# A table of steps for a four-segment attention and feed-forward kernel, with new first statistics, a new last inverse and a new last projection

## The chip, the core and the metric

The kernel runs on one core of a Trainium2 chip. Such a core has five engines with queues of their own that work in order and wait for each other through semaphores: TensorE (PE in the profile, with PEld for its weight loads), VectorE (DVE), ScalarE (ACT), GpSimd (POOL) and SyncE (SP, which here only issues DMAs). Operands lie in SBUF, 128 partitions wide. Products of TensorE go to PSUM, whose tiles VectorE and ScalarE read. The metric is the device time of one execution in microseconds (us).

## The reference

One sequence of 2048 rows and 448 columns is normalised row by row, and two branches read the result: an attention with a memory (16 heads of 28 columns, four segments of 512 rows), and a gated feed-forward layer with 1792 hidden columns. Inside a segment the attention is causal. The memory `M, z` is the sum over the segments before.

```
xn = layernorm(x)
for s in range(4):                          # per head, q, k, v = xn @ wq, wk, wv
    p = softmax(q_s k_s^T * scale + mask);  a_dot = p @ v_s
    a_mem = (phi(q_s) @ M) / (phi(q_s) @ z + 1e-6)      # phi(t) = t + 1 if t > 0 else exp(t)
    o_s = g * a_mem + (1 - g) * a_dot                   # g = sigmoid(beta), per head
    M += phi(k_s)^T v_s;  z += sum(phi(k_s))
s = concat(o_s) @ wo
out = x + s * silu((gelu(xn @ w_gate) * (xn @ w_up)) @ w_down)
```

## The kernel before

Everything is written out in one order by hand (a manual schedule), so the order in the code is each engine's order. A segment has four blocks of 128 rows (`b`), and its 16 heads are four groups (`g`) of four heads, each head padded from 28 to 32 partitions.

**Gate phases.** `gate_up(s)` runs over 14 chunks of 128 hidden columns. Each chunk is eight products into one of the two `ps_s` tiles, then a GELU on ScalarE (L511) and a product on VectorE (L512) that frees the tile. After each chunk the steps stand that a dictionary `table` gives for its number: statistics (`stats`, L241), scaling and transposing of the next segment, reading the memory (`memory_read`, L441), inverses of denominators (`invert`), and `scale_memory` and `combine`, which use them.

**Attention stages.** `attention(s, fill, at, lead)` takes a group in three steps (`BANKS`): key block 0 (512 query columns), key blocks 1 and 3 together (384 + 128 columns), and key block 2 alone (256 columns). A step is score products (L397), two exponentials on ScalarE (L403), masks of the diagonals on GpSimd (L407), and, two steps later, the products with the values (L418). Between steps a list `fill` of other TensorE work is dealt out by planned costs: projections of the next segment (L314, L352), the down projection (L523), and the products with `wo` (`finish_units`, L552). `at` gives steps to run at fixed half steps. `later(n, fn)` puts VectorE's half of a piece n ticks back.

**Inverses.** A group's accumulator is copied to SBUF (`evac`, L431). A DMA (L435) gathers the denominators of all groups into a small tile `dc`. `invert` computes the reciprocals there, splits each into three bf16 terms (L449 to L456), and three DMAs (L457) write these to `rows`. A product with a constant matrix `spread` (L465) then repeats every inverse over its head's partitions, and VectorE multiplies (L470, L481). In the last segment, groups 0 to 2 are inverted together, and group 3 afterwards, by the same way.

**The end.** After segment 3's attention the rest of its down projection runs, then the `wo` products of groups 0 to 2 for all four row blocks into two double tiles (L728), group 3's inverse and combination, its `wo` products, and per block a product (L738), an addition (L740) and a DMA out. In segments 0 to 2 GpSimd adds `x` and issues the output's DMA (L559, L560).

**The start.** 78 products of zeros (L93) run before the first data is there. VectorE takes the statistics of segment 0 (L241), GpSimd the power -1/2 (L247), VectorE scales, TensorE transposes (L265), ScalarE copies, and the value projection (L352) and then the key and query projections (L314) follow. `guard` squares the weights and sums the columns' squares by eight products (L218); a flag from this chooses the general path, which does not run here.

## Time and profile before

| what | value |
|---|---|
| median of 3 runs | 273.7 us (271.87 to 273.88) |
| the profiled execution's own time | 273.37 us |
| span in its trace, first to last instruction | 271.6 us |
| busy share of the span: PE, DVE, ACT, POOL | 92%, 70%, 57%, 37% |
| mean granted TensorE clock | 0.981 |

The span leaves 1.8 us of the execution's own time outside. The stages follow each other in the span: the start to 10.2 us, projections of segment 0 to 20.4, gate phase 0 to 45.0, attention 0 to 76.4, gate phase 1 to 103.5, attention 1 to 137.0, gate phases 2 and 3 to 187.0, attention 2 to 220.0, attention 3 to 245.6, and the end. The borders are read by eye from the chain of work, so a stage's edge can hold some of the next stage's instructions. Records of matmuls overlap, so a busy share of PE near one can still hold short waits.

### The profile page before, as it was taken

Reading aid. Unit: us, or ns where it says so; the run is one execution under the profiler, and the core shown is the slowest. Engines: PE = TensorE matmul, PEld = TensorE weight load, DVE = VectorE, ACT = ScalarE, POOL = GpSimd, SP = SyncE. Lnnn points to the kernel's source line nnn. Section 1 sums busy time; section 2 is a strip of 40 time slices with the busy share of each in tenths; the row PEclk is TensorE's granted clock in tenths of the full one; section 3 lists DMA queues with packets and bytes.
Section 4 is the critical chain, followed back from the end, with each engine's and each line's share of the span. In section 5 each row is a group of like instructions: output and inputs, shape, how many; then the busy total and the mean of one; then the engine's idle time right before and its main releaser. Section 6 shows DMA issues by size and latency. Waiting matters only on the chain.

```text
span 271.6 us, 4546 instructions
## 1 busy us (share of the span) xinstructions
PE 249.3 (92%) x1630; PEld 104.5 (38%) x1630; DVE 190.0 (70%) x371; ACT 155.5 (57%) x226; POOL 100.2 (37%) x203
## 2 busy tenths in 40 slices
PE   7899999999999999999999999999899998995940
PEld 7543334433333335444434333344333333332410
DVE  5876977667686878577778646355878756876862
ACT  2546735788985335688963332625887687871100
POOL 2100410455521400966622205121776563658011
PEclk9999999999999999999999999999999999999795
DMA  7999026020110143101110310002000010001002
GB/s 221 393 277 213 0 41 154 12 23 19 23 22 6 34 85 113 22 18 39 40 37 0 63 24 0 4 6 72 18 21 21 5 29 8 4 1 57 19 7 75
DMA packets 26358, 15.11 MB, mean 56 GB/s; under 512 B 17880, under 2 KB 25048, under 8 KB 26328
## 3 DMA queue, kind: packets, MB, share of 16 engines
q1 hardware_dynamic: 23032, 9.96, 16.7%
q10 hardware_dynamic: 2720, 3.40, 3.9%
q0 software_dynamic: 576, 1.38, 1.5%
q8 instruction: 15, 0.25, 0.4%
q14 instruction: 15, 0.12, 0.2%
HBM read 9.18 MB, written 1.84 MB: 41 GB/s over the span
## 4 chain that ended last, share of the span: by engine, by line
PE 66%; DVE 16%; ACT 6%; DMA 5%; issue 3%; POOL 1%; SPq 1%; DVEq 0%; ACTq 0%
PE s L496 22%; PE m L523 11%; PE m L314 9%; PE s L503 5%; PE s L397 5%; PE m L352 4%; PE pv L418 3%; ACT pt L403 3%; PE m L465 2%; DMA x_sb<-in_A_x_dram 2%; PE m L552 2%; DVE hT L512 2%; DMA rows<-terms 2%; PE m L441 1%; DMA dc<-oU 1%
## 5 line engine op out<-in xcount | busy, mean ns | idle before, releaser
L403 ACT ACTIVATE pt<-s 128x1024 bf16<-128x1024 f32 (+1 forms) x96 | 79.2, 885 | 16.8 <-PE s L397 16.3
L407 POOL TENSOR_SCALAR_AFFINE_SELECT pt<-pt 128x256 bf16<-128x256 bf16 x128 | 54.6, 449 | 71.5 <-ACT pt L403 70.0
L511 ACT ACTIVATE gl<-s 128x512 bf16<-128x512 f32 x56 | 33.4, 597 | 55.5 <-PE s L496 28.7
L512 DVE TENSOR_TENSOR hT<-gl,s 128x512 bf16<-128x512 bf16 x56 | 38.4, 685 | 31.4 <-ACT gl L511 31.3
L523 PE MATMUL m<-wd_sb,hT 128*128 128x448 bf16 x224 | 52.3, 361 | 0.9 <-DVE wu_sb L470 0.9
L496 PE MATMUL s<-xnT,wg_sb 128*128 128x512 bf16 x168 | 45.7, 381 | 1.2 <-DVE hT L512 1.2
L496 PE MATMUL s<-xnT,wu_sb 128*128 128x512 bf16 x168 | 45.4, 379 | 0.0
L523 PEld LDWEIGHTS <-hT 128*128 128x128 bf16 x224 | 20.7, 99 | 23.6 <-issue 6.8
L496 PEld LDWEIGHTS <-wu_sb 128*128 128x128 bf16 x168 | 16.4, 98 | 19.8
L397 PE MATMUL s<-qT,kT 32*128 32x512 bf16 (+3 forms) x256 | 20.9, 301 | 2.6 <-ACT pt L403 2.3
L496 PEld LDWEIGHTS <-wg_sb 128*128 128x128 bf16 x168 | 14.1, 97 | 22.2 <-issue 9.7
L247 POOL TENSOR_TENSOR rstd<-rstd,nhalf 128x2 f32<-128x2 f32 x8 | 5.7, 712 | 45.7 <-DVE rstd L245 45.7
L503 PE MATMUL s<-xnT,wg_sb 64*128 64x512 bf16 x112 | 19.4, 384 | 0.4 <-DVE hT L512 0.4
L318 DVE CAST kT<-m 128x512 bf16<-128x512 f32 x16 | 11.0, 688 | 11.2 <-PE m L314 11.0
L418 PE MATMUL pv<-pt,vaug 128*32 128x512 bf16 (+3 forms) x256 | 17.3, 307 | 0.0
L314 PE MATMUL m<-xnT,wk_pad 128*128 128x512 bf16 x64 | 17.1, 380 | 0.0
L314 PE MATMUL m<-xnT,wq_pad 128*128 128x512 bf16 x64 | 16.8, 380 | 0.2 <-DVE vaug L354 0.2
L397 PEld LDWEIGHTS <-kT 32*128 32x128 bf16 x256 | 6.5, 91 | 23.4 <-issue 23.1
L526 ACT ACTIVATE th<-m 128x448 f32<-128x448 f32 x16 | 8.8, 548 | 11.3 <-PE m L523 11.1
L352 PE MATMUL m<-wv_sb,xnT 128*128 128x448 bf16 x64 | 14.1, 352 | 0.6 <-DVE wu_sb L431 0.3
L465 PE MATMUL m<-rows,spread 128*128 128x512 bf16 x28 | 11.0, 391 | 3.1 <-DMA rows<-terms 2.6
L431 DVE COPY oU<-pv 128x512 f32<-128x512 f32 x13 | 8.9, 688 | 4.8 <-PE pv L418 4.8
(102 smaller groups left out, 305.7 us busy)
## 6 DMA issues: line engine op xcount, KB each, us to landing
x_sb<-in_A_x_dram SPq DMA_DIRECT2D x7, 224.0 KB
wd_sb<-in_B_w_down_dram SPq DMA_DIRECT2D x1, 1568.0 KB
wg_sb<-in_B_w_gate_dram SPq DMA_DIRECT2D x1, 1344.0 KB
wu_sb<-in_B_w_up_dram ACTq DMA_DIRECT2D x1, 1344.0 KB
out_dram<-o_out POOLq DMA_DIRECT2D x12, 112.0 KB, 2.1
xr<-in_A_x_dram ACTq DMA_DIRECT2D x2, 448.0 KB
wo_sb<-in_A_wo_dram SPq DMA_DIRECT2D x4, 98.0 KB
dc<-oU SPq DMA_DIRECT2D x24, 8.0 KB
```

Source lines behind the costliest of these rows:

```text
L314: nc.tensor.matmul(out=pr[:], lhsT=wpad[nm][:, c, g * HG:(g + 1) * HG, :].rearrange("p h d -> p (h d)"), rhs=xnT[s][:, c, :], start=(c == ...
L352: nc.tensor.matmul(out=vp[:, 0:D], lhsT=xnT[s][:, c, b * P:(b + 1) * P], rhs=wv_sb[:, c, :], start=(c == 0), stop=(c == NDC - 1))
L397: nc.tensor.matmul(out=sp[i // 2][:, i % 2, c0:c0 + n], lhsT=kT[s][r, g, kb * P:(kb + 1) * P], rhs=qT[s][r, g, kb * P:L], start=True, stop ...
L403: nc.scalar.activation(out=pt[:, :, 0:w], in_=sp[pr][:, :, 0:w], func=ACT.Exp, scale=scale)
L407: nc.gpsimd.affine_select(out=v, in_=v, pattern=[[0, 2], [1, P]], compare_op=ALU.is_ge, fill=0.0, base=0, channel_multiplier=-1)
L418: nc.tensor.matmul(out=acc[i * HP:(i + 1) * HP, kb * P:L], lhsT=va[:, kb, g * HG + i, :], rhs=pts[i // 2][:, i % 2, c0:c0 + n], start=(kb ...
L465: nc.tensor.matmul(out=r[:], lhsT=spread[:, g, :], rhs=rows[side][:], start=True, stop=True)
L496: nc.tensor.matmul(out=gu[:, i, :], lhsT=w_sb[:, c, cols], rhs=xnT[s][:, c, :], start=start and c == 0, stop=stop and c == NDC - 2)
L503: nc.tensor.matmul(out=gu[:, i, :], lhsT=wg_sb[rs, NDC - 1, cols], rhs=xnT[s][rs, NDC - 1, :], start=start, stop=stop)
L511: nc.scalar.activation(out=gl[:], in_=gu[:, 0, :], func=ACT.Gelu_apprx_tanh)
L512: nc.vector.tensor_tensor(out=hT[s][:, fc, :], in0=gl[:], in1=gu[:, 1, :], op=ALU.mult)
L523: nc.tensor.matmul(out=d_ps[:, 0:D], lhsT=hT[s][:, fc, b * P:(b + 1) * P], rhs=wd_sb[:, fc, :], start=(fc == 0), stop=(fc == NFC - 1))
```

## The change

One dictionary `PLAN` now says at which slot each named step runs. A slot is a gate chunk, a half step of an attention, or a unit of the last down projection; slots 0 to 13 are gate phase 0, 14 to 33 attention 0, 34 to 47 gate phase 1, 48 to 67 attention 1, 68 to 95 gate phases 2 and 3, 96 to 115 attention 2, 116 to 135 attention 3, and 136 onwards the end. Pairs such as `"v2": (0.031, 1.05)` say over which part of an attention a list of fill is spread, and other entries set delays and leads.

Beside the table:

- Two groups of heads share five attention steps instead of taking three each: the 256-column blocks of both go into one step. An attention has 10 steps, all 1024 columns wide for the exponentials.
- At the start ScalarE takes the statistics of blocks 2 and 3, GpSimd their power; 44 zero products instead of 78; `wv` is loaded before `wq`; memsets of `vaug` go to GpSimd; the value projection stands between the transposes.
- `guard` adds the squares on GpSimd, so that two products remain of eight; they stand in attention 0.
- Additions of `x` and output DMAs of segments 0 to 2 go from GpSimd to VectorE and SyncE. Three of the four `wo` units of segment 2 stand after attention 3.
- The last group's inverse: four f32 products with `pick` bring the denominators to the rows' partitions, VectorE inverts and spreads them, and four f32 products with `unit` turn them back. Its memory part is no longer added in `combine` but enters `wo` as a fifth source `om`.
- The last `wo` products run block by block, and GpSimd adds three of the four blocks.

```diff
+PLAN = {
...
+    "end30": 137, "end31": 137, "inv3": 138, "inv3l": 139, "cmb00": 42, "cmb10": 78, "cmb20": 126,
...
-        for i in range(78):
+        for i in range(44):
...
-                for c in range(NDC):
-                    nc.tensor.matmul(out=np_[0:1, 0:D], lhsT=ones[:], rhs=sqs[nm][:, c, :],
-                                     start=(c == 0), stop=(c == NDC - 1))
+                nc.tensor.matmul(out=np_[0:1, 0:D], lhsT=ones[:], rhs=sqs[nm][:, 0, :],
+                                 start=True, stop=True)
...
+            def stats_scalar(b):
+                junk = work.tile([P, D], BF16, name="ph_e")
+                nc.scalar.activation(out=junk[:], in_=xs[:, b, :], func=ACT.Copy, accum_out=mv[:, b, 0:1])
+                nc.scalar.activation(out=mv[:, b, 0:1], in_=mv[:, b, 0:1], func=ACT.Copy, scale=-1.0 / D)
+                nc.scalar.activation(out=junk[:], in_=xs[:, b, :], func=ACT.Square, bias=mv[:, b, 0:1],
+                                     accum_out=mv[:, b, 1:2])
...
-        BANKS = (((0, 0),), ((1, 0), (3, 384)), ((2, 0),))
+        STEPS = []
+        for a in range(0, G, 2):
+            b = a + 1
+            STEPS += [[(a, 0, 0)], [(a, 1, 0), (a, 3, 384)], [(a, 2, 0), (b, 2, 256)],
+                      [(b, 0, 0)], [(b, 1, 0), (b, 3, 384)]]
...
+        def invert_last():
+            o_a, d = oU[NSEG - 1, G - 1, 0], ps_m.tile([P, NB, HG], F32, name="m")
+            for b in range(NB):
+                nc.tensor.matmul(out=d[:, b, :], lhsT=o_a[:, b * P:(b + 1) * P], rhs=pick[:],
+                                 start=True, stop=True)
+            nc.vector.reciprocal(out=lden[:], in_=d[:])
...
+        def combine_last():
+            o_a, r = oU.pop((NSEG - 1, G - 1, 0)), ps_m.tile([P, L], F32, name="m")
+            for b in range(NB):
+                nc.tensor.matmul(out=r[:, b * P:(b + 1) * P],
+                                 lhsT=linv[:, b, :], rhs=unit[:], start=True, stop=True)
+            for h in range(2):
+                c = slice(h * L // 2, (h + 1) * L // 2)
+                nc.vector.tensor_tensor(out=oT[NSEG - 1][:, G - 1, c], in0=o_a[:, c], in1=r[:, c],
+                                        op=ALU.mult)
...
-                    nc.gpsimd.tensor_tensor(out=o_out[:], in0=t, in1=xr[s][:, b, :], op=ALU.add)
-                    nc.gpsimd.dma_start(out=o_v[s][:, b, :], in_=o_out[:])
+                    nc.vector.tensor_tensor(out=o_out, in0=t, in1=xr[s][:, b, :], op=ALU.add)
+                    nc.sync.dma_start(out=o_v[s][:, b, :], in_=o_out)
...
+        rest = d3[x:]
+        n = plan["fin_at"]
+        rest[n:n] = fin[w:]
...
-        for g in range(G - 1):
-            wo_part(g)
-        combine(3, G - 1, 1)
-        wo_part(G - 1)
+        combine_last()
+        srcs = [(om[0], G - 1)] + [(oT[3][:, g, :], g) for g in range(G)]
+        for b, a, z in ((0, 0, G), (1, 0, G), (0, G, G + 1), (1, G, G + 1), (2, 0, G + 1), (3, 0, G + 1)):
+            for n in range(a, z):
+                src, g = srcs[n]
+                nc.tensor.matmul(out=acc[b // 2][:, b % 2, 0:D], lhsT=src[:, b * P:(b + 1) * P],
+                                 rhs=wo_sb[:, g, :], start=(n == 0), stop=(n == G))
...
-            add = nc.vector if b % 2 else nc.gpsimd
+            add = nc.gpsimd if b < 3 else nc.vector
```

How the instructions stand now, at three places. A row is line, operation, output, inputs and shape; numbers behind a name tell buffers apart.

ScalarE at the start, after its table load, before (`oT` holds the raw `wk` here, `wu_sb` is the up weight, `m` a PSUM tile):

```order
L68 DMA oT<-in_A_wk_dram 128x3x448
L69 DMA oT<-in_A_wk_dram 64x448
L138 DMA wu_sb<-in_B_w_up_dram 128x3x1792
L139 DMA wg_sb<-in_B_w_up_dram 64x1792
L120 COPY wq_pad<-oT 128x64x28
L266 COPY xnT<-m 128x4x128 x4
```

ScalarE at the same place, in the changed kernel (`mv` holds mean and variance):

```order
L91 DMA oT_169<-in_A_wk_dram 128x3x448
L92 DMA oT_169<-in_A_wk_dram 64x448
L321 ACTIVATE ph_e_211,mv_204<-x_sb_105 128x448
L322 ACTIVATE mv_204<-mv_204 128x1
L323 ACTIVATE ph_e_211,mv_204<-x_sb_105,mv_204 128x448
L321 ACTIVATE ph_e_215,mv_204<-x_sb_105 128x448
```

The up weight's DMAs left this queue for SyncE's, the statistics of block 2 and then 3 came in, and the padding of `wq` went behind the copies of the transposes.

ScalarE in attention 2, four steps in the middle, before (`pt` are the exponentials, `s` the scores):

```order
L403 ACTIVATE pt_2570<-s_2564 128x1024
L403 ACTIVATE pt_2573<-s_2565 128x1024
L403 ACTIVATE pt_2615<-s_2605 128x1024
L403 ACTIVATE pt_2619<-s_2606 128x1024
L403 ACTIVATE pt_2650<-s_2644 128x2x256
L403 ACTIVATE pt_2653<-s_2645 128x2x256
L403 ACTIVATE pt_2674<-s_2668 128x1024
L403 ACTIVATE pt_2677<-s_2669 128x1024
```

ScalarE in attention 2 of the changed kernel, steps in the middle:

```order
L489 ACTIVATE pt_2536<-s_2530 128x1024
L489 ACTIVATE pt_2539<-s_2531 128x1024
L489 ACTIVATE pt_2577<-s_2567 128x1024
L489 ACTIVATE pt_2581<-s_2568 128x1024
L489 ACTIVATE pt_2620<-s_2610 128x1024
L489 ACTIVATE pt_2624<-s_2611 128x1024
```

The narrow pair is gone: two of them, from two groups, make one pair of full width.

VectorE's last rows before (`oU0_3198` is group 3's accumulator, `wg_sb` the feed-forward factor of segment 3, `s` the sums of `wo` products, `wv_sb` the output):

```order
L530 SCALAR_TENSOR_TENSOR wg_sb_2333<-th_3266,m_3250 128x448
L481 TENSOR_TENSOR oU0_3198<-oU0_3198,m_3283 128x512
L482 TENSOR_TENSOR oT_3208<-oU0_3198,wu_sb_2334 128x512
L738 TENSOR_TENSOR wg_sb_2333<-wg_sb_2333,s_3269 128x448 x2
L740 TENSOR_TENSOR wv_sb_3291<-wg_sb_2333,x_sb_1369 128x448
L738 TENSOR_TENSOR wg_sb_2333<-wg_sb_2333,s_3270 128x448 x2
```

VectorE's last rows in the changed kernel (`m_3205` is the last group's inverses, spread):

```order
L663 SCALAR_TENSOR_TENSOR wg_sb_2299<-th_3200,m_3176 128x448
L590 TENSOR_TENSOR oT_3161<-oU0_3104,m_3205 128x256 x2
L926 TENSOR_TENSOR wg_sb_2299<-wg_sb_2299,s_3203 128x448 x2
L926 TENSOR_TENSOR wg_sb_2299<-wg_sb_2299,s_3204 128x448 x2
L928 TENSOR_TENSOR wv_sb_3232<-wg_sb_2299,x_sb_1347 128x448
```

The last group's addition went, its product is in two halves, and one addition of two is left to VectorE.

## Rows read from the trace of the kernel before

**Rows 1.** Windows by stage: stretch, length, each engine's busy time (instructions), granted clock, DMA.

```profile
45.00:76.40 31.40, 30.96 (x241) 13.10 (x240) 20.92 (x38) 26.05 (x38) 15.40 (x33) 1.00 0.19 37
...
103.50:137.00 33.50, 33.50 (x259) 14.57 (x257) 25.19 (x41) 26.70 (x37) 21.03 (x40) 1.00 0.15 38
137.00:187.00 50.00, 49.59 (x259) 19.52 (x258) 30.32 (x59) 20.42 (x34) 11.84 (x20) 1.00 0.10 19
187.00:220.00 33.00, 31.33 (x242) 12.23 (x244) 24.66 (x43) 26.44 (x34) 20.62 (x42) 1.00 0.11 33
220.00:245.60 25.60, 23.20 (x198) 8.85 (x195) 19.24 (x36) 19.00 (x25) 13.57 (x32) 1.00 0.02 4
245.60:257.40 11.80, 8.93 (x40) 3.79 (x37) 8.98 (x18) 1.58 (x3) 4.92 (x7) 0.86 0.14 43
257.40:271.60 14.20, 3.59 (x18) 1.48 (x16) 6.28 (x9) 0.54 (x1) 2.06 (x2) 0.75 0.14 40
```

**Rows 2.** Groups by line and form: busy us, mean ns, idle before and releaser.

```profile
L403 ACT ACTIVATE pt<-s 128x1024 bf16<-128x1024 f32 x64 | 62.0, 1024 | 15.8 <-PE s L397 15.3 <-POOL pt L407 0.5
...
L403 ACT ACTIVATE pt<-s 128x512 bf16<-128x512 f32 x32 | 17.6, 608 | 1.0 <-PE s L397 1.0
```

**Rows 3.** Timeline of the start: begin, us, engine, line, operation, count.

```profile
1.59 6.23 PE L93 MATMUL pv<-wz 128*128 128x128 bf16 x78 [1.59 <-POOL wz L91]
...
3.94 0.63 DVE L241 BATCH_NORM_STATS2 st<-x_sb 128x6 f32<-128x448 bf16 x1 [1.81 <-DMA x_sb<-in_A_x_dram]
...
6.55 0.40 DVE L251 TENSOR_SCALAR xn<-x_sb,mv,rstd 128x448 bf16<-128x448 bf16 x1
...
6.96 1.69 ACT L120 COPY wq_pad<-oT 128x1792 bf16<-128x1792 bf16 x1 [4.13 <-DVE xn L251]
...
8.18 0.77 POOL L247 TENSOR_TENSOR rstd<-rstd,nhalf 128x2 f32<-128x2 f32 x1 [1.67 <-DVE rstd L245]
...
8.46 0.44 PE L265 MATMUL m<-ident,xn 128*128 128x128 bf16 x4 [0.43 <-DVE xn L251]
...
10.23 3.19 PE L352 MATMUL m<-wv_sb,xnT 128*128 128x448 bf16 x16
...
13.26 1.03 PE L314 MATMUL m<-xnT,wk_pad 128*128 128x512 bf16 x4
```

**Rows 4.** The chain that ended last: begin, us, what.

```profile
36.00 1.60 PE m L218 x8
...
108.13 0.57 PE m L523 x3
```

**Rows 5.** Timeline of the end.

```profile
243.13 0.42 DVE L449 TENSOR_SCALAR dc<-dc,igate 96x64 f32<-96x64 f32 x1 [0.71 <-DMA dc<-oU]
...
245.35 0.29 PE L418 MATMUL pv<-pt,vaug 128*32 128x256 bf16 x4
...
245.43 1.45 DVE L456 TENSOR_TENSOR dc<-dc,terms 96x64 f32<-96x64 f32 x1
...
245.74 1.04 POOL L559 TENSOR_TENSOR o_out<-sg,x_sb 128x448 bf16<-128x448 f32 x1
...
249.30 0.38 PE L465 MATMUL m<-rows,spread 128*128 128x512 bf16 x1 [2.61 <-DMA rows<-terms]
...
252.15 5.42 PE L523 MATMUL m<-wd_sb,hT 128*128 128x448 bf16 x22
...
255.49 0.22 DVE L456 TENSOR_TENSOR dc<-dc,terms 32x64 f32<-32x64 f32 x1
...
257.41 2.43 PE L728 MATMUL s<-wo_sb,oT 128*128 128x448 bf16 x12
...
262.15 1.15 DVE L738 TENSOR_TENSOR wg_sb<-wg_sb,s 128x448 f32<-128x448 f32 x2 [0.65 <-PE s L728]
...
265.47 1.03 DVE L740 TENSOR_TENSOR wv_sb<-wg_sb,x_sb 128x448 bf16<-128x448 f32 x1
```

**Rows 6.** Source view of line 339: duration ns least/median/most, first and last start.

```profile
L339 DVE SCALAR_TENSOR_TENSOR pkT<-kT,ph_e x8: 691/874/1405, 54.4 to 135.3; 128x512 bf16<-128x512 bf16 x8
```

418 lines of the change are left out of this document (264 added, 154 removed), and 18 rows, old and new, of the table PLAN.

## The prediction

> **What bounds the kernel now.** I read the windows by stage first, because the change touches every stage and each has its own limit [rows 1]. TensorE is busy 30.96 of 31.40 us in attention 0 and 33.50 of 33.50 in attention 1: these two are TensorE's, with ScalarE close behind (26.05 and 26.70). The gate phases are TensorE's too (49.59 of 50.00 in gate phases 2 and 3). Attention 2 (33.00 us) and attention 3 (25.60 us) belong to nobody: TensorE shows 31.33 and 23.20, though these overlap short waits, ScalarE 26.44 and 19.00, and VectorE 24.66 and 19.24. There engines wait for each other in turns. The group of wide exponentials says the same: ScalarE stood idle 15.8 us before them, 15.3 of it for scores from TensorE [rows 2].
>
> Then the end. From 245.6 to 257.4 TensorE is busy 8.93 of 11.80 us, at a mean granted clock of 0.86 [rows 1]. The timeline shows why [rows 5]: the inverses of groups 0 to 2 begin at 243.13 and the first `spread` product comes at 249.30, 2.61 us of it TensorE's idle wait for the DMA. After that wait the granted clock falls, to its lower level of 1.2 GHz for part of the stretch, and 22 down products take 5.42 us where three take 0.57 elsewhere, 0.19 each [rows 4, 5]. From 257.41 on the chain is serial: `wo` products, the last group's inverse, and VectorE's products and additions, until 266.50 (265.47 and 1.03) [rows 5]. The remaining 5.1 us to the span's end are the last output DMAs and the program's end, and I leave them as they are.
>
> The sum is made against the profiled execution's 273.4 us, which is 0.3 under the median of 273.7.
>
> **The change part by part.**
>
> *Start, -0.3.* The value projection begins at 10.23 and the key projection at 13.26 [rows 3]. In the changed order VectorE has the data at 3.94, makes two statistics (0.63 each, and two small operations behind each, together about 2.0), and two scalings of 0.40 and a little, so block 0 is turned at about 7 and its value product could begin near 8. It does not stay that early: four powers of 0.77 follow each other on GpSimd, so blocks 2 and 3 are scaled only at about 9 to 9.5, and since there are three PSUM tiles `m`, the transposes of block 3 need the tile of the first value product, whose copy stands on VectorE behind those scalings and the padding of `wk`. I come to a key projection at about 13.0. If these copies are not in the way, the gain is 1.4; if the padding of `wq` (1.69), now behind ScalarE's copies, ends after its products ask for it, the start loses up to 1.5.
>
> *Guard, -0.8.* Eight products took 1.60 us on the chain that ended last [rows 4]. Two remain, 0.4. Six fewer are 1.2; I count 0.8, because the two now stand in attention 0 before two reductions on VectorE, and the bounds are 0 and -1.2. The sums of squares on GpSimd lie beside gate phase 0, where nothing waits for it.
>
> *Attentions 0 and 1, -0.8.* A stage had 16 wide exponentials and 8 narrow ones, 16 x 1.024 + 8 x 0.608 = 21.2 us; it now has 20 wide ones, 20.5 [rows 2]. ScalarE wins 0.77 a stage. But TensorE is full there [rows 1], and its work is the same but for two step changes fewer of twelve. I take 0.4 a stage; the bounds are nothing, and 0.77 over ScalarE's share of 0.81, which is 1.9 for both.
>
> *Attentions 2 and 3, -4.5.* Together they take 58.6 us, ScalarE busy 45.4 of it, 77.5% [rows 1]. With 1.5 less, 43.9 us remain. At the same share that is 56.6 (-2.0); at attention 0's share, 26.05 of 31.40 or 83%, it is 52.9 (-5.7). Three things speak for the better half: every step is now equally long on ScalarE, one of the two `scale_memory` products that stood early in attention 2 goes back to gate phase 3, and three `wo` units leave attention 3 against one down unit that comes, 9 products of 0.19 or 1.7 us [rows 4]. I take 54.1. What is late next is the TensorE queue itself, at 31.33 of 33.00 with the waits it hides.
>
> *Additions of `x` on VectorE, 0.* Twelve additions of about 1.04 leave GpSimd, and twelve come to VectorE at up to 1.03 each [rows 5]. Eight fall into attentions 1 and 2, where VectorE stands idle 8.3 us in each [rows 1], and nothing waits for the output. They also take something away: beside GpSimd's two-input additions VectorE's own were stretched, a subtraction from 0.22 to 1.45 us [rows 5], a phi of keys from 0.69 to 1.41 [rows 6]. Three such phis in attention 1 give back about 2.1 of the 4.1 us. If that cover is gone, each addition stands ahead of a PSUM read and costs its 1.03: a rival below. The Trainium skill (SBUF — State Buffer, "Who interferes with whom") says that a VectorE instruction with two SBUF inputs and a GpSimd one that reads SBUF exclude each other for the whole instruction. The stretched rows agree, and by that rule the moved additions now meet GpSimd's masks instead.
>
> *Gate phases, 0.* Steps change places among the chunks, in equal number, and TensorE is already full [rows 1]. Bounds: a wait or two more, +1, or those at the edges gone, -1.5.
>
> *From attention 3's last value product to the last down product, -2.3.* This stretch took 11.8 us. In the changed order it holds 30 down products and 12 `wo` products at 0.19 [rows 4], 8.0 us, three `spread` products at no more than 0.38 [rows 5], 1.1, and four f32 products of four columns. No f32 product is in this trace; the nearest rows are four bf16 products of 128 columns in 0.44 [rows 3], so these cost 0 to 0.4. The sum is 9.5, if the wait is covered. The inverse took 6.2 us from its first operation to the `spread` product; without GpSimd's addition beside it the stretched subtraction (1.45 against 0.22) is 1.2 shorter, so 5.0. It began 2.5 us before the last value product ended (245.64) [rows 5]; placed alike, the rows are ready 2.5 us after it. TensorE has 20 products and the small ones in front, 4.2 us. The cover is 1.7 us thick, no wait is left, and with it the fall of the clock goes (22 products, 5.42 against 4.18). Bounds: 0 if the wait returns whole, -2.7.
>
> *From there to the last addition, -2.2.* Before: 257.41 to 266.50, 9.1 us [rows 5]. Now: four f32 products of 128 columns, between 0.44 [rows 3] and four times a 512-column one, 1.5 [rows 5]; I take 0.9. Eight `wo` products of blocks 0 and 1 hide VectorE's two halves of the last combination: 2.4. Two more: 2.8. Blocks 2 and 3, five each: 3.7 and 4.7. VectorE's products (1.15 for two [rows 5]) end at 3.3, 3.8, 4.4 and 5.3, its addition at 6.3; GpSimd's three (1.04 each) end at 6.4. That is 2.7 less; I take 2.2, since VectorE reaches its halves behind the last feed-forward factor. Bounds: -1 and -2.7. The Trainium skill (FP8 and Floating Point Precision, "TensorE Precision Notes") gives true FP32 four passes. By that the four cost an estimated 1.8 and the sum ends 0.9 later; no run shows it yet.
>
> Sum: 0.3 + 0.8 + 0.8 + 4.5 + 2.3 + 2.2 = 10.9, so 273.4 - 10.9 = **262.5 us**.
>
> **The rivals.** *Only the named parts act.* The table moves waits from one place to another, as TensorE's full rows in attentions 0 and 1 allow. Then start, guard and end remain: 5.6, so 267.8.
>
> *The table does all it could.* Every term at its better bound: 1.4 + 1.2 + 1.9 + 5.7 + 1.5 + 2.7 + 2.6 = 17.0, so 256.4. For it speaks that attentions 2 and 3 have no engine that is full; against it, that TensorE's busy time there already reaches 31.33 and 23.20.
>
> *VectorE becomes the bound.* Its queue is in order, and the reads that free the three PSUM tiles stand in it, so an addition ahead of such a read holds up TensorE for its whole length. With all twelve exposed and no gain from the table: 273.4 - 5.6 + 12 x 1.03 = 280.2. It ends slower than before once some six of the twelve are exposed. Against it stand VectorE's 75% in attentions 1 and 2, and the stretched operations that become short.
>
> *The clock falls at the start.* 78 zero products took 6.23 us, until the first transposes; 44 end 2 to 3 us earlier [rows 3], and then TensorE has only small pieces until the value products. At the end of the kernel such a thinning was followed by 0.86 [rows 1]. If the projections that follow run partly at 1.2 GHz, 1.2 us (the loss there) to 5 us (half of their ten): I take 2.5, so 265.0.
>
> **How the numbers follow.** The forecast gets 0.45, only the named parts 0.20, all the table could 0.20, the clock 0.10, VectorE as the bound 0.05. The range reaches from all but the last of the better bounds, 256.5, to the named parts with one of them failing, 269.5. About 1%, 2.7 us, is what a measurement of this kernel tells from no change. All of the first three and the clock lie below 271.0, except for a part of the named parts' case in which the inverse's wait stays and the start loses: faster 0.87, same 0.08, slower 0.05.
>
> **What would show it.** Right: ScalarE's exponentials as 80 equal ones; attentions 2 and 3 near 54 us with ScalarE over 80% busy; no wait for `rows` at the end and a granted clock of one until the last `wo` products; the last addition 6.4 to 7 us after the last down product; the first key projection near 13. Wrong: VectorE near full in attentions 1 and 2 with TensorE waiting for its casts; a `spread` product that waits in any phase; a granted clock below one in the first 20 us; or f32 products that take longer than 1.5 us for four.

## The result, and the profile after

The changed kernel takes 262.18 us (median of 4 runs, 261.74 to 262.56) beside 273.79 us of the kernel before (4 runs, 271.87 to 274.49). The ratio is 0.9586, with a 95% interval from 0.9535 to 0.9637. The profiled execution took 261.97 us, its span is 260.2 us, and its mean granted clock is 0.988.

The first view is the windows by stage of the changed kernel, columns as in [rows 1]. The borders are now drawn alike for every kernel: first and last GELU of gate phase 0 (the first from the load of its table on), the same of gate phase 1, of gate phases 2 and 3 together, the end of the last value product, and the end of the last down product. They are borders of ScalarE's queue, so TensorE's work can cross them.

```profile
20.42:44.42 24.00, 22.67 (x112) 8.73 (x112) 17.80 (x39) 13.00 (x19) 7.37 (x7) 1.00 0.52 97
44.42:74.50 30.08, 29.61 (x237) 12.47 (x235) 21.81 (x45) 26.50 (x36) 14.20 (x33) 1.00 0.14 31
74.50:100.65 26.15, 26.15 (x136) 9.60 (x135) 19.88 (x44) 12.05 (x20) 4.37 (x13) 1.00 0.18 32
100.65:133.28 32.63, 32.35 (x252) 14.29 (x252) 26.61 (x47) 26.66 (x35) 16.39 (x34) 1.00 0.22 57
133.28:185.93 52.65, 51.24 (x270) 19.88 (x268) 32.07 (x59) 20.48 (x34) 11.08 (x18) 1.00 0.08 16
185.93:237.23 51.30, 50.07 (x417) 19.32 (x416) 40.07 (x76) 44.03 (x50) 28.04 (x64) 1.00 0.09 25
237.23:247.01 9.78, 9.65 (x56) 5.57 (x56) 9.51 (x22) 1.62 (x3) 0.00 (x0) 1.00 0.13 39
247.01:260.20 13.19, 4.68 (x28) 2.58 (x27) 5.66 (x10) 0.55 (x1) 3.02 (x3) 0.77 0.13 41
```

The middle of the kernel before, with the same borders (attention 0, attention 1, gate phases 2 and 3):

```profile
46.43:77.71 31.28, 30.84 (x241) 12.84 (x239) 21.09 (x36) 26.62 (x39) 15.69 (x33) 1.00 0.15 28
...
103.98:137.98 34.00, 34.00 (x264) 14.65 (x266) 26.02 (x42) 26.85 (x37) 21.80 (x42) 1.00 0.15 41
137.98:187.70 49.72, 49.31 (x257) 19.53 (x257) 29.49 (x57) 20.38 (x34) 11.07 (x18) 1.00 0.09 17
```

The 11.4 us between the two spans lie as follows (the last addition ends at 266.50 before and at 254.03 now):

| stretch | before | after | difference | forecast |
|---|---|---|---|---|
| start, to the first GELU | 21.50 | 20.42 | -1.08 | -0.3 |
| gate phase 0 | 24.93 | 24.00 | -0.93 | -0.8 (guard) |
| attentions 0 and 1 | 31.28 + 34.00 | 30.08 + 32.63 | -2.57 | -0.8 |
| gate phase 1 | 26.27 | 26.15 | -0.12 | 0 |
| gate phases 2 and 3 | 49.72 | 52.65 | +2.93 | 0 |
| attentions 2 and 3 | 57.94 | 51.30 | -6.64 | -4.5 |
| last value product to last down product | 11.93 | 9.78 | -2.15 | -2.3 |
| from there to the last addition | 8.93 | 7.02 | -1.91 | -2.2 |
| from there to the span's end | 5.10 | 6.17 | +1.07 | 0 |
| sum | 271.6 | 260.2 | -11.40 | -10.9 |

The last row but one is not put down to the change: in the profiled executions below it lies between 4.5 and 6.8 us with the same end of the program. Stages are therefore compared up to the last addition. The median of before was 273.7 to 274.2 in the later comparisons, so that medians of different ones compare to some 0.4 us.

The group of exponentials, as in [rows 2], shows what was planned: 80 of one form, and ScalarE's idle time before them down to 13.1 us.

```profile
L489 ACT ACTIVATE pt<-s 128x1024 bf16<-128x1024 f32 x80 | 77.5, 1023 | 13.1 <-PE s L483 9.9
```

The timeline of the start answers to [rows 3]. The first value product comes 2.4 us earlier than before, though the third and fourth wait 0.62 us for VectorE's copy; the first key projection is at 12.18 (13.26 before).

```profile
1.59 4.25 PE L117 MATMUL pv<-wz 128*128 128x128 bf16 x44 [1.59 <-POOL wz L115]
...
4.42 0.58 ACT L321 ACTIVATE ph_e<-x_sb 128x448 bf16<-128x448 bf16 x1 [1.59 <-DMA x_sb<-in_A_x_dram]
...
7.84 0.93 PE L431 MATMUL m<-wv_sb,xnT 128*128 128x448 bf16 x4
...
10.67 1.67 PE L431 MATMUL m<-wv_sb,xnT 128*128 128x448 bf16 x8 [0.62 <-DVE vaug L433]
...
12.18 1.03 PE L392 MATMUL m<-xnT,wk_pad 128*128 128x512 bf16 x4
```

The timeline of the end answers to [rows 5]. The first operation of the inverse takes 0.25 us beside no GpSimd (0.42 before), its subtractions 0.22 each (1.45 for one before), the `spread` product at 242.04 has no idle time in front of it (2.61 before), and the windows above show a granted clock of 1.00 up to the last down product, where it was 0.86. The additions at the bottom are one on VectorE beside three on GpSimd.

```profile
236.79 0.25 DVE L541 TENSOR_SCALAR dc<-dc,igate 96x64 f32<-96x64 f32 x1 [0.79 <-DMA dc<-oU]
...
237.93 1.79 SPq L549 DMA_DIRECT2D rows<-terms  x2
...
238.31 0.95 PE L571 MATMUL m<-pick,oU 128*128 128x4 f32 x8
...
238.62 0.19 DVE L546 CAST terms<-dc 96x64 bf16<-96x64 f32 x1
...
242.04 0.38 PE L560 MATMUL m<-rows,spread 128*128 128x512 bf16 x1
...
246.85 1.05 PE L586 MATMUL m<-unit,macc 128*128 128x128 f32 x8
...
250.54 3.02 POOL L928 TENSOR_TENSOR wv_sb<-wg_sb,x_sb 128x448 bf16<-128x448 f32 x3 [13.72 <-DVE wg_sb L926]
...
252.91 1.13 DVE L928 TENSOR_TENSOR wv_sb<-wg_sb,x_sb 128x448 bf16<-128x448 f32 x1
```

### The profile page after: what moved, and what is told of

Read it like the earlier page. It is cut to its first block, busy times and chain, and to the rows that moved or that the text cites. A ratio compares the mean times of both kernels' runs of the same rounds, so it can differ in the third digit from the quotient of the medians.

```text
span 260.2 us, 4481 instructions
## 1 busy us (share of the span) xinstructions
PE 243.5 (94%) x1609; PEld 102.7 (39%) x1609; DVE 187.5 (72%) x373; ACT 157.3 (60%) x220; POOL 93.0 (36%) x196
## 3 DMA queue, kind: packets, MB, share of 16 engines
q10 hardware_dynamic: 2204, 1.79, 2.3%
## 4 chain that ended last, share of the span: by engine, by line
PE 71%; DVE 12%; ACT 6%; DMA 3%; issue 2%; POOL 1%; ACTq 0%; DVEq 0%
PE s L627 23%; PE m L653 13%; PE m L392 10%; PE s L634 5%; PE s L483 5%; PE pv L502 4%; PE m L431 3%; PE m L688 3%; ACT pt L489 2%; DVE hT L643 2%; PE m L560 2%; PE s L921 1%; DMA pkb<-pqT 1%; ACT gl L642 1%; DMA x_sb<-in_A_x_dram 1%
## 5 line engine op out<-in xcount | busy, mean ns | idle before, releaser
L489 ACT ACTIVATE pt<-s 128x1024 bf16<-128x1024 f32 x80 | 77.5, 1023 | 13.1 <-PE s L483 9.9
L493 POOL TENSOR_SCALAR_AFFINE_SELECT pt<-pt 128x256 bf16<-128x256 bf16 x128 | 56.5, 462 | 66.3 <-ACT pt L489 63.4
L653 PE MATMUL m<-wd_sb,hT 128*128 128x448 bf16 x224 | 50.2, 353 | 0.0
L295 POOL TENSOR_TENSOR rstd<-rstd,nhalf 128x2 f32<-128x2 f32 (+1 forms) x8 | 5.4, 676 | 41.8 <-DVE rstd L293 41.8
L483 PE MATMUL s<-qT,kT 32*128 32x512 bf16 (+3 forms) x256 | 19.1, 300 | 1.1 <-ACT pt L489 0.5
L392 PE MATMUL m<-xnT,wq_pad 128*128 128x512 bf16 x64 | 17.5, 380 | 0.0
L502 PE MATMUL pv<-pt,vaug 128*32 128x128 bf16 (+3 forms) x256 | 15.9, 305 | 0.0
L483 PEld LDWEIGHTS <-kT 32*128 32x128 bf16 x256 | 5.5, 91 | 18.5 <-issue 18.2
L634 PEld LDWEIGHTS <-wg_sb 64*128 64x128 bf16 x112 | 5.2, 93 | 19.1 <-issue 18.5
L546 POOL CAST terms<-dc 128x64 bf16<-128x64 f32 x12 | 3.0, 249 | 24.5 <-DVE dc L543 24.0
```

Of the source, the lines that this page charges most:

```text
L392: nc.tensor.matmul(out=pr[:], lhsT=wpad[nm][:, c, g * HG:(g + 1) * HG, :].rearrange("p h d -> p (h d)"), rhs=xnT[s][:, c, :], start=(c == ...
L483: nc.tensor.matmul(out=sp[i // 2][:, i % 2, c0:c0 + n], lhsT=kT[s][r, g, kb * P:(kb + 1) * P], rhs=qT[s][r, g, kb * P:L], start=True, stop ...
L489: nc.scalar.activation(out=pt[:, :, 0:w], in_=sp[pr][:, :, 0:w], func=ACT.Exp, scale=scale)
L493: nc.gpsimd.affine_select(out=v, in_=v, pattern=[[0, 2], [1, P]], compare_op=ALU.is_ge, fill=0.0, base=0, channel_multiplier=-1)
L502: nc.tensor.matmul(out=acc[i * HP:(i + 1) * HP, kb * P:L], lhsT=vaug[s % 2][:, kb, g * HG + i, :], rhs=pts[i // 2][:, i % 2, c0:c0 + n], s ...
L634: nc.tensor.matmul(out=gu[:, i, :], lhsT=wg_sb[rs, NDC - 1, cols], rhs=xnT[s][rs, NDC - 1, :], start=start, stop=stop)
```

## Experiments

Twelve kernels ran, in three groups, each group on one chip with the kernel before. The changed kernel did not run again in them, so a difference from it goes from one group to another.

### The attentions: packing, its buffers, the table

`steps12`, the changed kernel without the packing:

```diff
-        for a in range(0, G, 2):
-            b = a + 1
-            STEPS += [[(a, 0, 0)], [(a, 1, 0), (a, 3, 384)], [(a, 2, 0), (b, 2, 256)],
-                      [(b, 0, 0)], [(b, 1, 0), (b, 3, 384)]]
+        for a in range(G):
+            STEPS += [[(a, 0, 0)], [(a, 1, 0), (a, 3, 384)], [(a, 2, 0)]]
...
-                    go()
+                    if 20 * n // 24 > 20 * (n - 1) // 24:
+                        go()
```

> The changed kernel with the packing of the attention steps undone: three steps per group again (1024, 1024 and 512 columns), 12 a stage, the table's 20 slots spread over the 24 half steps; everything else stays. Theory (the prediction's terms for the attentions, -0.8 and -4.5, come from the packing): most of 5.3 us return, 266 to 268, with ScalarE's wide exponentials at x64 and narrow ones at x32 again, and attentions 2 and 3 some 4 us longer than their 51.3. Rival (the table brought it, by where it puts the other steps; the packing is worth no more than ScalarE's own 0.77 us a stage where ScalarE is not full): at most 1 us returns, 262 to 263.2. A middle value would say how much of the packing is beyond the table.

`b_packed`, the kernel before with the packing alone (steps, score and value products taken over from the changed kernel):

```diff
-            at, done, n = dict(at or {}), 0.0, 0
-            steps, pts, acc = [(g, bk) for g in range(G) for bk in range(3)], {}, {}
+            old, at, done, n = dict(at or {}), {}, 0.0, 0
+            for h in sorted(old):
+                at.setdefault(h * 20 // 24, []).extend(old[h])
+            steps, pts, acc, put_off = STEPS, {}, {}, []
```

> The kernel before with one part of the change alone: the ten packed steps per attention; its own fixed steps keep their places in proportion (half step h of 24 becomes h x 20 / 24), and nothing else is changed. Theory (the packing makes the attentions' gain): 273.8 - 5.3 = 268.5, most of it in attentions 2 and 3, which take 57.9 us before. Rival (the table made it): 273.8 less at most 1, 272.8 to 274; a third reading, that equal steps need the new places to be of use, would show as no change here and a loss where the changed kernel's packing is undone.

`steps12` took 269.65 us (ratio to before 0.9846, 0.9805 to 0.9888), 7.5 more than the changed kernel. `b_packed` took 277.36 us, slower than before (1.0109, 1.0054 to 1.0164). So the packing is worth more than forecast with the table, and nothing without it, the third reading of the second text. That `b_packed` is slower lies mostly at its end: from the last value product to the last down product it takes 14.16 us (11.93 before), since the inverse of groups 0 to 2 begins late and a `spread` product waits 4.44 us for `rows`; the four stages compared below are 0.6 longer. The waits of ScalarE in `b_packed` name one cause why the stages gain nothing (us in total, times, longest): it waited for value products, that is, for a buffer of exponentials to come free.

```profile
ACT pt L407 <- PE s L401: 13.5, 19, 1.8
...
ACT pt L407 <- PE pv L420: 5.1, 4, 3.1
```

The pool of these buffers had grown from 6 to 8 in the change, a line that neither the list of the change above nor the prediction names. Two kernels test it, in both directions, with `pool("ptp", 8)` in `b_packed` and `pool("ptp", 6)` in the changed kernel:

```diff
-        ptp = pool("ptp", 6)
+        ptp = pool("ptp", 8)
```

> The kernel before with the packed steps and with eight buffers for the exponentials (the pool ptp) instead of six, as the changed kernel has; two buffers pkT instead of three and the update's product in the tile th make the room. Theory (packing needs the buffers: a packed pair is held until its second group's accumulator is free, and ScalarE waited 5.1 us for value products with six): that wait goes, attentions 2 and 3 fall from 58.2 to about 55 and the whole from 277.4 to 273 to 275. Rival (the fixed steps stand wrongly for ten steps, and the wait only changes its name): 276.5 or more. In both the end stays 2.2 us longer than before, since the inverse of groups 0 to 2 began late in the packed order.

> The changed kernel with six buffers for the exponentials instead of eight, nothing else. Theory (the two buffers are part of what the packing gives): ScalarE waits for value products again, 3 to 5 us over four attentions, and TensorE behind it: 264 to 267. Rival (the table's places leave the buffers time enough): 262.0 to 262.7.

`a_ptp6` took 266.77 us (0.9736, 0.9698 to 0.9774), 4.6 more than the changed kernel. Some of that is the clock: in two of its four executions the mean granted clock is 0.988 and 0.989, and they take 267.2 us; in the other two it is 0.993 and 0.994, and they take 266.3. Its waits have the line that the changed kernel's lack:

```profile
ACT pt L489 <- PE s L483: 12.1, 14, 2.6
ACT pt L489 <- PE pv L502: 4.9, 5, 2.5
```

`b_packed8` took 276.48 us (1.0091, 1.0059 to 1.0122). There the wait for buffers is gone, but it only changed its name, as the rival had it: 13.5 and 5.1 became

```profile
ACT pt L407 <- PE s L401: 18.1, 22, 3.1
```

So scores came late in the old order, whatever the buffers. `a_even` asks whether that is the dealing of the fill (the leads of attentions 0 to 2 are set to 2.6 too):

```diff
...
-    "lead3": 0.42, "upd0": (0.02, 0.233), "v0": (0.068, 0.299), "down0": (0.277, 1),
+    "lead3": 0.42, "upd0": (0, 0.18), "v0": (0, 0.18), "down0": (0.18, 1),
...
-    "qk1": (0.122, 0.721), "fin1": (0.303, 1.05), "v2": (0.031, 1.05), "qk2": (0.082, 0.998),
+    "qk1": (0.16, 1), "fin1": (0.16, 1), "v2": (0, 1), "qk2": (0, 1),
```

> The changed kernel with the table's entries for the fill of attentions 0 to 2 set as the kernel before dealt it: every list spread evenly over the whole stage (the update and the value projections ahead of the rest in 0 and 1), lead 2.6; steps at fixed slots, packing and buffers stay. Theory (where the fill stands decides whether packed steps gain, which is why packing alone in the kernel before gave nothing, with eight buffers too): attentions 2 and 3 grow from 51.3 to 54 or more, 265 to 268. Rival (the fixed steps, scalings and combinations moved to gate phases 2 and 3, and the three wo units moved behind the last attention decide it): 262 to 263.

It took 266.16 us (0.9692, 0.9662 to 0.9722), as the theory had it, but not at the place that the theory named. The stages of all seven kernels, with the borders of above:

| kernel | attention 0 | attention 1 | gate phases 2, 3 | attentions 2, 3 | sum |
|---|---|---|---|---|---|
| before | 31.28 | 34.00 | 49.72 | 57.94 | 172.9 |
| packing alone, 6 buffers | 30.43 | 35.15 | 49.78 | 58.20 | 173.6 |
| packing alone, 8 buffers | 30.06 | 35.24 | 49.77 | 57.93 | 173.0 |
| changed, no packing | 32.83 | 34.41 | 52.40 | 55.19 | 174.8 |
| changed, 6 buffers | 30.40 | 32.95 | 52.62 | 56.53 | 172.5 |
| changed, fill dealt evenly | 31.57 | 35.24 | 52.63 | 52.03 | 171.5 |
| changed | 30.08 | 32.63 | 52.65 | 51.30 | 166.7 |

Attention 0 gains from the packing alone. Attention 1 gains only when the fill is dealt as the table does it: 35.24 with packing and even dealing in either kernel, 32.63 with the table's. Attentions 2 and 3 need the eight buffers (5.2 us, with a fall of the clock in the profiled execution among them) and the packing (3.9 us), and the fill's dealing is worth only 0.7 there. With packing, buffers and even dealing they take 52.03 in the changed kernel and 57.93 in the old one; what is left between these is the fixed steps' places, the three `wo` units behind attention 3, and work that moved into gate phases 2 and 3. In the old order the three `wo` units alone shorten these stages by 1.2 (`b_fin_late` below, 56.78); the other two no run takes apart. The table's slots were made for ten steps, so `steps12` may overstate the packing.

### The end

`end_dma`, the changed kernel with the last group's inverse by DMA, which begins two slots later (141 for 139):

```diff
-                put(f"inv{s}l", invert_last)
+                put(f"inv{s}l", lambda: invert(s, 0, G - 1, G, 1, **quick))
...
-            o_a, r = oU.pop((NSEG - 1, G - 1, 0)), ps_m.tile([P, L], F32, name="m")
-            for b in range(NB):
-                nc.tensor.matmul(out=r[:, b * P:(b + 1) * P],
-                                 lhsT=linv[:, b, :], rhs=unit[:], start=True, stop=True)
+            o_a, r = oU.pop((NSEG - 1, G - 1, 0)), inverses(NSEG - 1, 0, G - 1, 1)
```

> The changed kernel with the last group's inverse by DMA again: its denominators go out by a DMA, are inverted and split as for the other groups, come back by three DMAs and are spread by one product; the pick and unit products (8 and 8 records, 0.95 and 1.05 us) and the spread inverse on VectorE are gone; the last wo products stay block by block. Theory (the wait at the end went because products stand behind the last attention, not because of the way the inverse takes): about 6 us of DMA, VectorE and DMA fit into the 9.8 us between the last value product and the last down product, so there is no wait for rows, and TensorE has 1.6 us less to do: 260.5 to 262.2. Rival (taking DMA out of the last inverse removed the wait): the last spread product waits 1.5 us or more and the granted clock falls as before, 264 to 266.

262.46 us (0.959, 0.9544 to 0.9636): no change that the medians can tell, and 0.3 above the theory's range. To the last addition the trace shows 0.74 us more (254.77 against 254.03). The rival's wait is not there; the first `spread` product waits 0.23 us, and later a `wo` product waits 0.96 us, since the longer inverse on VectorE delays the combinations:

```profile
238.30 1.78 SPq L547 DMA_DIRECT2D rows<-terms  x2
...
241.44 0.38 PE L558 MATMUL m<-rows,spread 128*128 128x512 bf16 x1 [0.23 <-DMA rows<-terms]
...
249.03 0.36 PE L915 MATMUL s<-wo_sb,oT 128*128 128x448 bf16 x1 [0.96 <-DVE oT L609]
```

`b_fin_late`, the kernel before with three `wo` units of segment 2 moved behind attention 3. Their additions follow at once, and the combinations and the last group's inverse stand three units later, so that they keep their places between the down products:

```diff
-        ends = attention(3, d2[8:] + d3[:6] + finish_units(2), at, lead=0.6)
+        fin = finish_units(2)
+        ends = attention(3, d2[8:] + d3[:6] + fin[:1], at, lead=0.6)
...
-        for n, u in enumerate(d3[6:]):
+        for n, u in enumerate(d3[6:8] + fin[1:] + d3[8:]):
```

> The kernel before with one part of the change alone: three of the four wo units of segment 2 stand after attention 3, ahead of the first spread product; its additions on GpSimd follow them at once. Theory (cover): the 12 products (0.19 us each, 2.3 in all) fill the 2.61 us wait for rows, the granted clock stays at one through the down products (22 in about 4.2 instead of 5.42), and attention 3 is shorter by up to 2.3 us: 273.8 - 1.2 to -3.5, 270.3 to 272.6, and the stretch from the last value product to the last down product grows by less than 1.2 us. Rival (the inverse is later by as much, since its start or its VectorE steps move along, with GpSimd's additions beside them): the wait stays over 1.5 us and the clock falls: 273.8 or more.

272.95 us (0.9963, 0.9943 to 0.9983, with 10 runs of it): 1.2 less than the 274.1 of before in this group. That is 0.3 above the theory's span and 0.8 below the rival's least, so the total alone decides little; the trace does. In the windows of its last two stretches before the outputs the first shows the clock at 1.00, where it was 0.86, and it holds the 12 `wo` products more, in 11.23 us where the old one took 11.93:

```profile
244.56:255.79 11.23, 9.70 (x51) 4.72 (x50) 9.66 (x19) 1.67 (x3) 6.40 (x8) 1.00 0.14 45
255.79:264.72 8.93, 3.42 (x18) 1.38 (x15) 7.08 (x11) 0.54 (x1) 2.05 (x2) 0.82 0.10 29
```

To the last addition that is 1.8 us (264.72 against 266.50). The first `spread` product has no wait in front of it. Some of the gain is eaten by GpSimd's additions, which now stand here: beside one of them, at 249.07, a product of VectorE took 1.70 us, and the third `spread` product waited 1.32.

```profile
248.97 1.70 DVE L482 TENSOR_TENSOR oT<-oU,wu_sb 128x512 bf16<-128x512 f32 x1
249.07 1.04 POOL L559 TENSOR_TENSOR o_out<-sg,x_sb 128x448 bf16<-128x448 f32 x1
...
251.25 0.38 PE L465 MATMUL m<-rows,spread 128*128 128x512 bf16 x1 [1.32 <-DVE wg_sb L530]
```

`add_pool`, the changed kernel with the additions of `x` on GpSimd (`nc.vector` to `nc.gpsimd`, `nc.sync` to `nc.gpsimd` in `rest` of `finish_units`):

> The changed kernel with the twelve additions of x and their output DMAs on GpSimd again. Prediction's term: 0, so 261.5 to 262.9. Rival 1 (GpSimd's two-input additions stretch VectorE's work beside them, as the scalings above): phis of keys of 1.4 us again, and the inverse at the end later; 263.5 to 266. Rival 2 (the additions cost VectorE 0.61 each on the path): 258 to 261.

261.22 us (0.9538, 0.9501 to 0.9576), 0.3 below the range of the term of 0 and above rival 2. The trace says otherwise: to the last addition it takes 0.7 us more (254.70 against 254.03), and only the rest of the span is shorter (4.53 against 6.17). So the term of 0 holds to less than a microsecond, and its sign stays open. Attentions 2 and 3 stay within 0.2 us (51.10). At the end the trace shows what the move is good for: 10.60 us for the stretch of 9.78, with the inverse's first operation stretched and a `wo` product waiting behind it:

```profile
236.47 1.03 POOL L696 TENSOR_TENSOR wq_pad<-sg,x_sb 128x448 bf16<-128x448 f32 x1
236.49 1.07 DVE L541 TENSOR_SCALAR dc<-dc,igate 96x64 f32<-96x64 f32 x1 [1.32 <-DMA dc<-oU]
...
239.91 1.67 PE L688 MATMUL m<-wo_sb,oT 128*128 128x448 bf16 x8 [0.95 <-DVE sg L691]
```

### The start and the guard

`zeros20`: `range(44)` to `range(20)`.

> The changed kernel with 20 products of zeros at the start instead of 44; they end 2.3 us earlier, at about 3.5, and TensorE is then idle for some 3 us before the first transposes. The prediction's rival on the clock: the granted clock falls below one during the first projections, which costs 1.2 to 5 us, 263 to 267. Theory: at the start nothing of the kind happens for so short a pause, and the time stays, 261.7 to 262.7.

261.99 us (0.9555, 0.9522 to 0.9588): no change. TensorE stands idle from 3.9 to 6.3 us, and the column of the granted clock stays at 1.00 in every window behind it. The rows say more than the column. The first four products of the value projection take 1.68 us, where they take 0.93 in the changed kernel, and only from 9.55 on are they as quick as there:

```profile
7.67 1.68 PE L431 MATMUL m<-wv_sb,xnT 128*128 128x448 bf16 x4
...
9.55 0.92 PE L431 MATMUL m<-wv_sb,xnT 128*128 128x448 bf16 x4
...
12.22 1.03 PE L392 MATMUL m<-xnT,wk_pad 128*128 128x512 bf16 x4
```

The products of zeros show the same. In the changed kernel they start 0.107 us apart until about 5.0 us and 0.056 apart from then on; here all 20 start 0.107 apart. So with 20 of them TensorE works at half its rate, that of the lower level of 1.2 GHz, until about 9.5 us, although the column gives 1.00. It costs nothing, since the changed kernel's later value products wait 0.62 us for VectorE's copy: the first key projection is at 12.22 here and at 12.18 there.

`vec_stats`, all first statistics on VectorE:

```diff
-            for b in (2, 3):
-                stats_scalar(b)
-            for b in (0, 1):
-                stats(b)
-            for b in (2, 3):
-                power_scalar(b)
+            for b in range(NB):
+                stats(b)
```

> The changed kernel with all four first statistics on VectorE, one after the other; ScalarE's statistics and GpSimd's small operations for them are gone, the rest of the start stays. Theory (the split lets blocks 2 and 3 be scaled early, and their transposes, whose PSUM tiles the value products share, come early; this is most of the 1.08 us that the start gave): two statistics of 0.63 and their small operations stand ahead of the scalings of block 0 or behind, the first value product comes 1.5 to 2 us later and the first GELU 1 to 2 us later: 263.2 to 264.2. Rival (the start's gain came from the order of the copies and loads and from fewer zeros): 262 to 262.6.

262.79 us (0.9575, 0.9547 to 0.9602), 0.6 more, between theory and rival. The profiled execution was its longest, 263.71; in its trace the first GELU is 2.28 us later (the load of its table at 22.70) and the last addition 1.8. Not all of that is the queue on VectorE. The zeros, at the quick rate from about 5.6 us on, had ended at about 6.1, the transposes begin at 8.39, and then the granted clock falls to its lower level, 1.2 GHz, which it does not do in the changed kernel (windows of 1 us, columns as in [rows 1]):

```profile
8.00:9.00 1.00, 0.54 (x6) 0.37 (x7) 1.00 (x6) 0.00 (x0) 0.89 (x2) 1.00 0.98 359
9.00:10.00 1.00, 1.00 (x6) 0.47 (x6) 1.00 (x4) 0.48 (x1) 0.89 (x5) 0.50 1.01 401
...
12.00:13.00 1.00, 1.00 (x8) 0.57 (x7) 0.68 (x2) 0.17 (x1) 0.93 (x2) 0.80 0.99 237
```

`guard8`, the sums of squares by eight products again (`for c in range(NDC)`, and GpSimd's additions of squares left out):

> The changed kernel with the sums of the weights' squares on TensorE again, eight products and not two, at their new place in attention 0; GpSimd's additions of squares are gone. Prediction's term: 0.8, bounds 0 and 1.2, so 262.6 to 263.4, with attention 0 longer by six products of 0.2. Rival (TensorE's queue has the room in attention 0, the gain in gate phase 0 came from the place): 262.0 to 262.4.

262.37 us (0.9563, 0.9536 to 0.9591). The median lies in the rival's range and can't be told from the changed kernel's. The trace can: attention 0 takes 31.19 us against 30.08, 1.11 for six products, and the last addition ends 0.97 later (255.00). The cost that the prediction gave six products stands, near its upper bound.

### A step of the table moved

`turn_early`: `"turn32": 78` to `"turn32": 77`. In the changed kernel's timeline of gate phase 2 the second scaling of a block stood beside GpSimd's additions, and took 0.97 and 1.24 us where the one before took 0.40 and 0.29; TensorE then waited:

```profile
152.26 0.40 DVE L301 TENSOR_SCALAR xn<-x_sb,mv,rstd 128x448 bf16<-128x448 bf16 x1 [0.22 <-POOL rstd L295]
...
154.13 2.53 POOL L614 TENSOR_TENSOR oT<-oU,oU 128x512 bf16<-128x512 f32 x2 [1.91 <-DVE oU L613]
...
154.57 0.97 DVE L301 TENSOR_SCALAR xn<-x_sb,mv,rstd 128x448 bf16<-128x448 bf16 x1
...
155.46 1.24 DVE L304 TENSOR_SCALAR xn<-x_sb,mv,rstd 128x64 bf16<-128x64 bf16 x1
...
157.34 0.39 PE L634 MATMUL s<-xnT,wg_sb 64*128 64x512 bf16 x2 [1.28 <-DVE hT L643]
```

> The changed kernel with one entry of the table moved: block 2 of segment 3 is scaled and turned one slot earlier, ahead of two products of combine and GpSimd's two additions behind them. There VectorE's two scalings took 0.97 and 1.24 us instead of 0.40 and 0.29, a product hT came late and TensorE waited 1.28 us for it, in a stretch (gate phases 2 and 3) that is 2.9 us longer than before. Theory (the scalings were stretched by GpSimd's additions beside them): they take 0.4 and 0.3 again, the wait goes, 260.9 to 261.4. Rival (VectorE's queue is only rearranged and the wait comes a chunk later): 262.0 to 262.6.

260.43 us (0.9523, 0.9483 to 0.9562), the fastest of all and 0.5 below the theory's range. Gate phases 2 and 3 take 51.32 us against 52.65, and the scalings of both blocks are short, ahead of GpSimd's additions, which begin at 154.26:

```profile
152.39 0.39 DVE L301 TENSOR_SCALAR xn<-x_sb,mv,rstd 128x448 bf16<-128x448 bf16 x1
152.69 0.30 DVE L304 TENSOR_SCALAR xn<-x_sb,mv,rstd 128x64 bf16<-128x64 bf16 x1
...
154.26 2.50 POOL L614 TENSOR_TENSOR oT<-oU,oU 128x512 bf16<-128x512 f32 x2 [2.42 <-DVE oU L613]
...
154.69 0.68 DVE L643 TENSOR_TENSOR hT<-gl,s 128x512 bf16<-128x512 bf16 x1
```

What stands beside the additions now is the product `hT`, one of whose inputs lies in PSUM, and it takes 0.68 us there, as elsewhere. The Trainium skill (SBUF — State Buffer, "Who interferes with whom") says that a `tensor_scalar` of VectorE can run in a mode with two ports, and that of such an instruction and a GpSimd one the later waits for the whole of the earlier. The stretched scalings agree with that, and the stretching went with the neighbour.

## Why the prediction was right, and where its steps were not

The time came out 0.3 us from the forecast, and the terms have the right signs but for the gate phases, forecast at 0. But three sizes are outside their bounds, two for the better and one for the worse. These stages exchange work, so their errors cancel in large part: attentions 0 to 3 and gate phases 1 to 3 together gave 6.4 us, where 5.3 was forecast. This and the start gave 1.9 us more than the forecast, and that the time lies so near it is in good part luck: 1.07 us more stand behind the last addition, for a reason that no run here shows.

**Attentions 0 and 1 (-0.8 forecast, -2.57).** Outside the bounds, but the two stages do not hold the same work before and after. In attention 1 TensorE has 264 records before and 252 after. By their starts, eight value products, four gate products and a `spread` product fewer lie between the borders, and two products of the value projection more. The gate and `spread` products at their spacing (0.15 to 0.22 us) and the 0.31 us of value products that the gate phases gained make an estimated 0.9 of the 1.37 us, work that now stands behind the stage. The rest, about 0.5, is near the 0.4 forecast. So this stage does not refute "TensorE is full there" [rows 1]: packing with even dealing made it longer (35.24), and the dealing of the table, which the prediction had left among the rivals, gave back 2.61. In attention 0 the step did fail. `b_packed8` has the same 241 products there as the kernel before and takes 30.05 us instead of 31.28. A busy time of 30.84 of 31.28 was no floor: it holds the changes between steps, and waiting counts in it too. `a_ptp6` takes 0.30 us more in attention 0 than the changed kernel with the same 237 records, and all of it shows as busy (29.91 of 30.38 against 29.61 of 30.08).

**Attentions 2 and 3 (-4.5, -6.64), gate phases (0, +2.81).** ScalarE's share rose as forecast: 44.03 of 51.30 us are 86%, where over 80% was asked for. But equal steps alone do not raise it: `b_packed8` has the same 80 equal exponentials and eight buffers, and stays at 57.93 us and 76%. The sizes are off in both, and they belong together. Of the 2.93 us that gate phases 2 and 3 grew, 1.33 was the wait that `turn_early` took away, a wait by contention that the prediction had put under "a wait or two more, +1". The rest is work that crossed a border (270 records against 257): by their starts eight value, four gate, three down, two `wo` products and a `spread` product more and three query products fewer, an estimated 1.6 us at the spacing of their rows. Out of attentions 2 and 3 went fourteen `wo` products (18 against 32), twelve of them behind attention 3, and a `spread` product, for three query products that came: an estimated 2.2 us net, where the prediction had 1.7. The other 4.4 are waits and step changes that went. Together the two stages gave 3.7 of 4.5. And the gain hangs on a line that the prediction passed over: with six buffers attentions 2 and 3 give only 1.4, and the kernel takes 266.8 us, 4.3 above the forecast.

**Start (-0.3, -1.08).** Mis-sized. The pieces were right (a first value product near 8, measured 7.84), but the powers of GpSimd took 0.55 to 0.65 us and not 0.77, and the copies on VectorE held up the value products by 0.62 once and not at every tile. The rival in which the clock falls did not come: the changed kernel's value products run at the quick rate from the first one on. With 20 zero products TensorE is at the lower level until about 9.5 us, and it still costs nothing, so the price of 1.2 to 5 us was too high there; the fall came in `vec_stats`, where the statistics weren't split.

**Guard (-0.8).** Right in the cost, 1.11 for six products, though at the new place. In gate phase 0, which all eight left, only 0.93 was won, while TensorE's waits for `hT` went from 0.8 to 1.4 us there; the two that came to attention 0 cost some 0.4.

**From the last value product to the last down product (-2.3, -2.15).** Right, for a reason thinner than stated. The cover was put at 1.7 us, with `rows` ready 2.5 us after the last value product. In `end_dma` the `spread` product waited for `rows` until 241.44; the last issue of the `rows` DMAs ended at 240.08 there (238.30 and 1.78) and at 239.72 in the changed kernel (237.93 and 1.79), 0.36 earlier, so `rows` was ready at an estimated 241.1, 3.9 after the last value product. The mis-sized step is "placed alike": the inverse began 0.44 us before the end of the last value product (236.79, 237.23) and not 2.5. From its first operation to `rows` it took an estimated 4.3 us, less than the 5.0 counted. The `spread` product comes at 242.04, so the cover was about 1.0 thick, and nearly all of that is a second mis-sizing: the four `pick` products, priced 0 to 0.4, took 0.95. That the products behind attention 3, and not the way of the last inverse, took the wait and the fall of the clock away is shown from both sides, by `b_fin_late` and `end_dma`.

**To the last addition (-2.2, -1.91).** Right; only the sum of all better bounds has 2.6 for this term's 2.7. The four `unit` products took 1.05 us, where 0.9 was taken. In the trace each f32 product is two weight loads and two matmuls; these start about 0.11 us apart, 0.22 for a product, which is four times the 0.056 between the starts of bf16 transposes of the same 128 columns. The `pick` products, of four columns, for the most part start as far apart, so it may be the weight loads (0.19 each, against 0.10 in bf16) that set it. The Trainium skill (FP8 and Floating Point Precision, "TensorE Precision Notes") gives true FP32 four passes, from which the prediction had an estimated 1.8. The measured 1.05 does not speak against four passes: the 1.8 is four times the 0.44 of four transposes, and 0.22 of the 0.44 is the length of the last one alone. The last inverse through TensorE as such is worth 0.7 us in the trace (`end_dma`).

**Additions on VectorE (0).** Right as far as the runs tell, to less than 1 us. They took 0.62 us (median; the longest of the twelve 0.83) and not the 1.03 of the upper price, and GpSimd's had taken 1.05; VectorE, at 26.61 of 32.63 us in attention 1, did not become the bound. The phis of keys went from 691, 874 and 1405 ns [rows 6] to 691, 693 and 877, but they did in `add_pool` too, so it wasn't this move that shortened them.

## What to carry to other kernels

A packing of steps and the order of the work around it are one change: alone, each of them gave nothing in the stages of the table above (173.0 and 174.8 us against 172.9), and together they took 6.2 us off, so a trial of one part says little about the whole. Packed steps hold their buffers longer; count the buffers of a pool before reading the waits. A TensorE that shows itself busy throughout can still be waiting; but before a shorter stage is called a gain, count the products on both sides of its borders. A scaling on VectorE is best put ahead of GpSimd's two-input additions and not beside them: one slot in the table was worth 1.3 us.

## What had not been expected

- The column of the granted clock does not show the start. In the changed kernel the products of zeros run at half the rate until about 5.0 us, and in `zeros20` TensorE does until about 9.5, both while the column gives 1.00. In `vec_stats`, where TensorE had come to the quick rate and then stood idle for 2.28 us, the column fell to 0.50 from 9 to about 12.4 us. That it did not fall in `zeros20` after an idle 2.37 us does not make the two cases differ: there had been no rise before it.
- ScalarE's statistics have a price beside the two passes: each `accum_out` is followed by an instruction of 0.19 us that reads the accumulator.
- With six buffers the granted clock of attentions 2 and 3 was 0.97 and not 1.00 (`a_ptp6`): it fell at about 218.4 us, after TensorE had waited 1.06 and 0.58 us for ScalarE. Such waits can cost a second time.
